# Two of sixteen weight pieces converted inside the last feed-forward instead of the expert slots

## The chip, the cores and the metric

One core of one Trainium2 chip runs the whole program. The metric is the device time of one execution in microseconds (us); the profile is one execution taken by the hardware profiler. TensorE is PE in the profile (PEld is its weight load), VectorE is DVE, ScalarE is ACT, GpSimd is POOL, SyncE is SP.

## The reference

Three layers follow each other. Attention over q, k, v (4 x 8 heads x 576 x 64) with a position bias gives x of 2304 x 512. A mixture of 8 experts sends each row to one expert:

```python
h = np.maximum(x[mask] @ w1[e], 0.0)
out[mask] = gate_w[mask, None] * (h @ w2[e])
```

The last feed-forward, with `w_in` 512 x 2048 and `w_out` 2048 x 512 that the host hands over as 64-bit floats, is

```python
r = np.maximum(x @ w_in, 0.0)
g = r * r
return (g @ w_out).astype(np.float32)
```

## The kernel before

**Stages.** Attention runs first. Then 22 expert slots (`run_slots`, L1283), each 128 rows of one expert; then the last feed-forward (L1381 to L1521) in 9 blocks of 256 rows. Matrix products are done in pairs of 16-bit halves: every operand has a high half and a low half, and a product is three products of halves.

**An expert slot.** PE does `ff1` for the next slot in two parts of 48 matmuls (L1220), transposes of x for the slot after it (L1203), and `ff2` of this slot, 24 matmuls (L1235). ACT and DVE make the halves of the results (L1225, L1226, L1243), and, where the expert changes, of the next first weight (`split_w1`, L1014 and L1015). POOL gathers rows and scatters results by DMA and splits x. SP loads first weights (L999, four DMAs of 512 KB), second weights (L1008, four DMAs of 512 KB into one buffer `vt`, each as soon as `ff2` has read the old quarter).

**The conversion in the slots.** The 64-bit weights have to become 16-bit halves. `convert(i, ...)` (L1101) does one of 16 pieces: pieces 0 to 7 are `w_in`, 8 to 15 are `w_out`. A `w_out` piece is a load of 1 MB by SP (L1109), then in this order Abs on ACT (L1116), a clamp and a shift on DVE (L1118, L1119), two bit operations on DVE (L1121, L1123), four subtractions on POOL (L1136) that make the 7 combinations of a fast 2 x 2 block product, the high half on ACT (L1140), the low half on DVE (L1142), and a store by SP into a DRAM buffer `wosc` (L1144). `pieces` (L1147) interleaves the pieces in steps, seven per piece; `piece(t, n)` (L1278), called four times per slot, issues steps until `1 + (t - 2 + 0.25 n) * CPACE` are done, with `CPACE` 6.1. All engines run their queues in the order written in the program.

**The last feed-forward.** SP loads the eight pieces of `w_out` from `wosc` into the resident tile `woh` (L1503). `g_unit(j, c)` (L1411) is one unit: PE makes two column groups of x @ w_in (24 matmuls, L1420) into one of four PSUM buffers, ACT does relu (L1426) into `gf`, of which there are two. Every second unit closes a pair: a square (L1431 on ACT in blocks 0 and 1, L1433 on DVE later), four adds on POOL (L1436), and then for the pair before it the high half on ACT (L1443) and the low half on DVE (L1444) into the block's tile `g2` (28 KB per partition, two buffers). `ff2_of(j)` (L1446) is the second product of block j, seven products of 24 matmuls (`prod`, L1454) that each run over all eight pieces of `woh`, piece 7 last. Its first product (`pf_a`) stands ahead of unit 13 (block 1, c = 5), the next two ahead of units 14 and 15, the other four after unit 15. So units 0 to 12 have no second product between them.

```python
if c > (2 if j > 1 else 4) and not (last and c == 6):
    next(two, None)
g_unit(j, c)
```

Of the kernel before, what the change touches and what calls it, by code (L numbers as in the profile page):

```python
# [7 lines left out]
F32 = mybir.dt.float32  # L8
F16 = mybir.dt.float16
U32 = mybir.dt.uint32  # L10
I32 = mybir.dt.int32
AF = mybir.ActivationFunctionType
ALU = mybir.AluOpType
# [10 lines left out]
P = 128  # L24
# [14 lines left out]
W1S, W2S, YS = 64.0, 64.0, 2.0 ** -8  # L39
WIS, RS, WOS = 64.0, 2.0 ** -8, 64.0  # L40
OUTS = 2.0 ** -22
CPACE = 6.1
NCONV, NWIN = 16, 8
HSW = 134
TINY64, HUGE = 2.0 ** -15 * 1.125, 3e38

# [37 lines left out]
def body(ctx: ExitStack, tc: tile.TileContext, q, k, v, wsm, emb, tau, mw1, mw2, win, wout, cst_d, lsk_d, ids_d, out):  # L84
    nc = tc.nc
    win, wout = win.bitcast(U32), wout.bitcast(U32)
    PE, ACT, DVE, POOL, SP = nc.tensor, nc.scalar, nc.vector, nc.gpsimd, nc.sync
# [863 lines left out]
    with tc.manual_schedule():  # L951
# [149 lines left out]
        def convert(i, wrp):  # L1101
            wr = wrp.tile([P, 1024, 2], U32, name="wr2", bufs=4)
            wf = wr.rearrange("p n t -> p (n t)")
            if i < NWIN:
                kc, n = divmod(i, 2)
                SP.dma_start(out=wf, in_=win[kc * P:(kc + 1) * P, n * 2048:(n + 1) * 2048])
            else:
                g = i - NWIN
                SP.dma_start(out=wf, in_=wout[g * P:(g + 1) * P, :])  # L1109
            lo, hi = wr[:, :, 0], wr[:, :, 1]  # L1110
            yield
            tb = wrp.tile([P, 8, 256], F32, name="tb", bufs=2)
            flat = tb.rearrange("p q n -> p (q n)")
            af, bf = flat[:, :1024], flat[:, 1024:]
            b = bf.bitcast(U32)
            ACT.activation(bf, hi.bitcast(F32), AF.Abs)  # L1116
            yield
            DVE.tensor_scalar(bf, bf, TINY64, None, op0=ALU.max)  # L1118
            DVE.tensor_scalar(b, b, 3, 0x3FFFFFF8, op0=ALU.logical_shift_left, op1=ALU.bitwise_and)  # L1119
            yield  # L1120
            DVE.scalar_tensor_tensor(out=b, in0=lo, scalar=29, in1=b, op0=ALU.logical_shift_right, op1=ALU.bitwise_or)  # L1121
            yield
            DVE.scalar_tensor_tensor(out=af.bitcast(U32), in0=hi, scalar=0xC0000000, in1=b,  # L1123
                                     op0=ALU.bitwise_and, op1=ALU.bitwise_or)
            yield
            if i < NWIN:
                yield
                dh, dl = (wih[:, a, kc, n * 1024:(n + 1) * 1024] for a in range(2))
                ACT.activation(dh, af, AF.Copy, scale=WIS)
                yield  # L1130
                DVE.scalar_tensor_tensor(out=dl, in0=af, scalar=WIS, in1=dh, op0=ALU.mult, op1=ALU.subtract)
                yield
                return
            for d, x, y, op in ((4, 0, 1, ALU.subtract), (5, 2, 4, ALU.subtract), (6, 2, 0, ALU.subtract),
                                (7, 3, 5, ALU.subtract)):
                POOL.tensor_tensor(out=tb[:, d], in0=tb[:, x], in1=tb[:, y], op=op)  # L1136
            yield
            wo = wf.bitcast(F16)[:, :2 * 7 * 256]
            dh, dl = wo[:, :7 * 256], wo[:, 7 * 256:]
            ACT.activation(dh, flat[:, 256:], AF.Copy, scale=WOS)  # L1140
            yield
            DVE.scalar_tensor_tensor(out=dl, in0=flat[:, 256:], scalar=WOS, in1=dh, op0=ALU.mult, op1=ALU.subtract)  # L1142
            yield
            SP.dma_start(out=wosc[:, g * 3584:(g + 1) * 3584], in_=wo)  # L1144


        def pieces(cs):  # L1147
            for c in cs[:4]:
                next(c)
            yield  # L1150
            next(cs[0])
            yield
            none = iter(())
            for n in range(len(cs) + 1):
                c, d = cs[n] if n < len(cs) else none, cs[n - 1] if n else none
                next(c, None)
                if 0 < n <= NWIN and n + 3 < len(cs):
                    next(cs[n + 3])
                yield
                next(d, None)  # L1160
                yield
                next(c, None)
                yield
                next(d, None)
                if n > NWIN + 1 and n + 2 < len(cs):
                    next(cs[n + 2])
                yield
                next(c, None)
                yield
                next(c, None)  # L1170
                if n + 1 < len(cs):
                    next(cs[n + 1])
                yield
                next(d, None)
                yield
# [7 lines left out]
        wrp = ep("e_wr", 1)  # L1183
# [77 lines left out]
            DVE.tensor_copy(orow[:, i:i + 1], yr[:, DM + 1:XW])  # L1261


        conv = pieces([convert(i, wrp) for i in range(NCONV)])
        done = [0]
        state = ["tail"]
        yq, yd = [], []
# [10 lines left out]
        def piece(t, n):  # L1278
            while done[0] < (1 if t < 2 else 1 + (t - 2 + 0.25 * n) * CPACE):
                next(conv, None)  # L1280
                done[0] += 1
# [99 lines left out]
        with ExitStack() as fctx:  # L1381
            fp = lambda n, bufs, **kw: tp(fctx, n, bufs, **(kw if "space" in kw else dict(side="right")))
            woh = fp("f_wo", 1).tile([P, 8, 2, 7, 256], F16, name="woh")
            gp = fp("f_g", 2)
# [7 lines left out]
            gts, gfs, late, outs = {}, {}, [], []  # L1392
            yv = lambda j: y0[:, :, :, 256 * (j % 2):256 * (j % 2) + 256]

            def y_load(j):
                for i in range(2):
                    t = 2 * j + i
                    SP.dma_start(out=us_t[t % 4][:, :XW], in_=y_d[t * P:(t + 1) * P, :])
# [11 lines left out]

            def g_unit(j, c):  # L1411
                y2 = yv(j)
                if c == 0:
                    gts[j] = gp.tile([P, 2, 7, 8, P], F16, name="g2")
                p_ = pf1.tile([P, 2, 256], F32, name="pf1")
                for h in range(2):
                    f, i = 8 * h + c, 0
                    for kc in range(4):
                        for a, b in ((0, 0), (0, 1), (1, 0)):
                            PE.matmul(p_[:, h], lhsT=wih[:, a, kc, f * P:(f + 1) * P], rhs=y2[:, b, kc, :],  # L1420
                                      start=(i == 0), stop=(i == 11))
                            i += 1
                if c % 2 == 0:
                    gfs[j] = gfp.tile([P, 8, 2, P], F32, name="gf")
                g = gfs[j]
                ACT.activation(g[:, 0:4, c % 2, :], p_.rearrange("p h (i n) -> p (h i) n", i=2), AF.Relu, scale=RS)  # L1426
                if c % 2 == 0:
                    return
                g4 = g[:, 0:4].rearrange("p q c n -> p (q c n)")
                if j < 2:  # L1430
                    ACT.activation(g4, g4, AF.Square)  # L1431
                else:
                    DVE.tensor_tensor(out=g4, in0=g4, in1=g4, op=ALU.mult)  # L1433
                for d, x, y, op in ((4, 0, 2, ALU.add), (5, 4, 1, ALU.subtract), (6, 1, 0, ALU.subtract),
                                    (7, 3, 5, ALU.subtract)):
                    POOL.tensor_tensor(out=g[:, d], in0=g[:, x], in1=g[:, y], op=op)  # L1436
                g_split()
                late.append((g, gts[j], c - 1))

            def g_split():  # L1440
                while late:
                    g, gt, c = late.pop()
                    ACT.copy(gt[:, 0, :, c:c + 2, :], g[:, 1:8])  # L1443
                    DVE.tensor_tensor(out=gt[:, 1, :, c:c + 2, :], in0=g[:, 1:8], in1=gt[:, 0, :, c:c + 2, :], op=ALU.subtract)  # L1444
# [54 lines left out]
                put(0)  # L1499
                yield  # L1500

            for g in range(8):
                SP.dma_start(out=woh[:, g].rearrange("p a q n -> p (a q n)"), in_=wosc[:, g * 3584:(g + 1) * 3584])  # L1503
            for j in range(NB):
                two = ff2_of(j - 1) if j else iter(())
                last = j == NB - 1
                for c in range(8):
                    if c > (2 if j > 1 else 4) and not (last and c == 6):
                        next(two, None)
                    g_unit(j, c)  # L1510
                    if 0 < j < NB - 1:
                        if c == 0:
                            y_load(j + 1)
                        if c in (3, 5):
                            y_split(2 * (j + 1) + c // 2 - 1)
                if last:
                    g_split()
                for _ in two:
                    pass
# [68 lines left out]
```

## Time and profile before

| what | us |
|---|---|
| three timed runs, median (lowest to highest) | 1030.5 (1030.4 to 1036.81) |
| profiled execution, its own time | 1023.01 |
| span of the profiled execution | 1021.2 |
| PE busy in it | 949.9 (93%) |
| DVE, ACT, POOL busy | 657.3, 541.0, 500.6 |
| expert slots with conversion, by the trace | about 427 to 655 |
| units 0 to 12 of the last feed-forward | 655 to 689 |

The profiled execution lies 1.8 us above its span and 7.5 us below the median of the timed runs. PE's ends are modelled, so a busy PE is not a PE at its peak: how long a fixed number of matmuls takes is the better reading.

### The profile page before, as it was taken

What the parts mean: (1) busy time and instruction counts of PE and PEld (TensorE: products, weight loads), DVE (VectorE), ACT (ScalarE), POOL (GpSimd) and SP (SyncE); (2) the same over time, 40 slices, a digit from 0 to 9 for tenths busy, and PEclk for the clock granted to TensorE, in tenths of its full rate; (3) what the DMA queues carried; (4) which work ended last, traced back from release to release, by engine and by line L of the source; (5) the groups of instructions that cost most, each with busy time, mean ns of one, the idle gap of its engine ahead of it and who ended that gap; (6) DMA issues with size and microseconds to landing.
All of it is one profiled execution on the core that took longest, in us unless ns stands there. A gap on an engine that the chain in (4) does not pass through costs nothing. (4 is left out here: it accounts for less than half of the span.)

```text
span 1021.2 us, 24809 instructions
## 1 busy us (share of the span) xinstructions
PE 949.9 (93%) x9725; PEld 751.8 (74%) x9725; DVE 657.3 (64%) x1229; ACT 541.0 (53%) x1000; POOL 500.6 (49%) x415
## 2 busy tenths in 40 slices
PE   7587899999899889999989899999999999999995
PEld 4355676677677767776667677688888888888884
DVE  6665789899988764677866768235455555545441
ACT  5575677777877673466656564355333233333330
POOL 1212537356433352366638798266454654645541
PEclk9798999999999989999989999999999999999998
DMA  8989886898789334599899484371121111021001
GB/s 285 309 242 294 283 262 201 263 283 292 225 254 324 145 126 148 222 333 334 327 370 336 148 288 156 114 301 42 32 54 42 31 53 42 27 58 22 21 2 42
DMA packets 78843, 187.17 MB, mean 183 GB/s; under 512 B 26648, under 2 KB 26776, under 8 KB 76128
## 3 DMA queue, kind: packets, MB, share of 16 engines
q1 hardware_dynamic: 72656, 169.98, 49.8%
q0 software_dynamic: 6064, 15.54, 4.4%
q8 instruction: 78, 1.28, 0.5%
q14 instruction: 45, 0.37, 0.1%
HBM read 171.65 MB, written 51.73 MB: 219 GB/s over the span
## 5 line engine op out<-in xcount | busy, mean ns | idle before, releaser
L1436 POOL TENSOR_TENSOR gf<-gf 128x256 f32<-128x256 f32 x144 | 165.9, 1171 | 146.7 <-DVE gf L1433 124.4
L1420 PE MATMUL pf<-big,wih 128*128 128x256 f16 x1728 | 196.0, 273 | 1.8 <-PEq L1374 1.8
L1420 PEld LDWEIGHTS <-wih 128*128 128x128 f16 x1728 | 169.0, 98 | 21.8 <-issue 2.2
L1458 PEld LDWEIGHTS <-g 128*128 128x128 f16 x1512 | 147.4, 98 | 18.7 <-issue 1.0
L1426 ACT ACTIVATE gf<-pf 128x512 f32<-128x512 f32 x72 | 42.5, 597 | 193.6 <-PE pf L1420 138.0
L1220 PE MATMUL ph<-x,w1b 128*128 128x128 f16 x2112 | 127.1, 220 | 7.2 <-DVEq L1024 2.5
L1220 PEld LDWEIGHTS <-w1b 128*128 128x128 f16 x2112 | 121.7, 99 | 12.3 <-DVEq L1024 3.0
L471 POOL TENSOR_TENSOR wh<-wr,w2s_c 128x1024 f16<-128x1024 f32 x32 | 61.1, 1910 | 133.8 <-DMA wr<-in_mw_dram 71.1
L1235 PE MATMUL py<-vt,h 128*128 128x512 f16 x528 | 120.3, 385 | 5.3 <-DMA vt<-wsc 5.3
L522 ACT ACTIVATE pr<-ssb,mn 128x576 f32<-128x576 f32 x144 | 111.7, 776 | 12.8 <-DVE mn L509 12.5
L1444 DVE TENSOR_TENSOR g<-gf,g 128x1792 f16<-128x1792 f32 x36 | 85.5, 2374 | 50.3 <-ACT g L1443 50.3
L509 DVE CUSTOM_DVE_ANT_0 ssb<-ps_s,bias 128x576 f32<-128x576 f32 x144 | 107.4, 748 | 8.7 <-DMA bias<-bias_d 7.0
L498 PE MATMUL ps_s<-kst,qd 128*128 128x288 f16 (+1 forms) x640 | 97.4, 293 | 10.8 <-DVE mn L509 9.1
L1433 DVE TENSOR_TENSOR gf<-gf 128x1024 f32<-128x1024 f32 x28 | 34.3, 1225 | 113.6 <-ACT gf L1426 113.6
L1235 PEld LDWEIGHTS <-h 128*128 128x128 f16 x528 | 51.5, 99 | 65.3 <-issue 9.7
L531 PE MATMUL ps_t<-cst,pr 128*128 128x128 f32 x576 | 93.3, 286 | 1.2 <-DVE pt L209 1.0
L556 PE MATMUL pv<-pt,vt 128*64 128x128 f32 (+1 forms) x1280 | 85.5, 277 | 6.6 <-DMA vt<-in_v_dram 5.7
L556 PEld LDWEIGHTS pv<-pt,vt 128*64 128x64 f32 x1280 | 68.0, 142 | 23.3 <-issue 16.4
L531 PEld LDWEIGHTS ps_t<-cst,pr 128*128 128x128 f32 x576 | 65.7, 146 | 24.0 <-issue 19.8
L498 PEld LDWEIGHTS <-qd 128*128 128x128 f16 (+1 forms) x640 | 56.9, 102 | 26.0 <-issue 16.6
L1443 ACT CAST g<-gf 128x1792 f16<-128x1792 f32 x36 | 60.3, 1676 | 4.3 <-POOL gf L1436 4.3
L207 ACT COPY pt<-ps_t 128x512 f32<-128x512 f32 x99 | 57.0, 576 | 10.3 <-PE ps_t L531 10.2
(194 smaller groups left out, 1542.7 us busy)
## 6 DMA issues: line engine op xcount, KB each, us to landing
vt<-wsc SPq DMA_DIRECT2D x88, 512.0 KB
wr<-in_mw_dram SPq DMA_DIRECT2D x76, 512.0 KB
kst<-in_mw_dram SPq DMA_DIRECT2D x44, 512.0 KB
wsc<-wh SPq DMA_DIRECT2D x32, 512.0 KB
bias<-bias_d SPq DMA_DIRECT2D x16, 576.0 KB
bias_d<-rt SPq DMA_DIRECT2D x28, 295.5 KB
qd<-qh SPq DMA_DIRECT2D x64, 128.0 KB
wr<-in_win_dram SPq DMA_DIRECT2D x8, 1024.0 KB
```

What stands on the lines that cost most here:

```text
L471: POOL.tensor_tensor(out=wh[:, 0], in0=wr, in1=w2s_c.to_broadcast([P, 1024]), op=ALU.mult)
L498: PE.matmul(s[r, hf, :288], lhsT=qd[:, h2, i, pr, r], rhs=kst[x - x % 2][:, pr, h2, x % 2, js], start=(i == 0), stop=(i == 1))
L509: DVE.tensor_tensor_reduce(out=ss.rearrange("p (a j) -> p a j", a=2), in0=s[:, :, :288], in1=btile[bkey[u]][:, h2].rearrange("p (a j) -> p ...
L522: ACT.activation(pr_sb[k_ // 2][:, h2], ssb.pop(k_), AF.Exp, bias=mns.pop(k_), scale=-1.0, accum_out=sums[c, b][:, h:h + 1])
L531: PE.transpose(pt_ps[k_][:, jc * P:(jc + 1) * P], src[:, j0:j0 + P], eye)
L556: PE.matmul(pv[o, cs], lhsT=vb[:, 2 * jc + h2, d] if jc < 4 else vb[o, 8, d], rhs=a[h2][:, jc, cs] if jc < 4 else e[o, cs], start=(jc == 0 ...
L1220: PE.matmul(p_[:, f4, :], lhsT=w[:, a, kc, f * P:(f + 1) * P], rhs=x2[:, b, kc, :], start=(i == 0), stop=(i == 11))
L1235: PE.matmul(p_, lhsT=h2[:, a, fc, :], rhs=wb2[fc // 2][:, b, fc % 2, :], start=(i == 0), stop=(i == 23))
L1420: PE.matmul(p_[:, h], lhsT=wih[:, a, kc, f * P:(f + 1) * P], rhs=y2[:, b, kc, :], start=(i == 0), stop=(i == 11))
L1436: POOL.tensor_tensor(out=g[:, d], in0=g[:, x], in1=g[:, y], op=op)
L1444: DVE.tensor_tensor(out=gt[:, 1, :, c:c + 2, :], in0=g[:, 1:8], in1=gt[:, 0, :, c:c + 2, :], op=ALU.subtract)
L1458: PE.matmul(ps, lhsT=gt[:, a, s, c, :], rhs=woh[:, c, b, w, :], start=(i == 0 and first), stop=(i == 23 and end), skip_group_check=True)
```

## The change

The last two pieces of `w_out` (6 and 7 of 8) are taken out of the slots; the other 14 pieces are spread over the same slots with `CPACE` 5.4. The two are loaded raw into the second `g2` buffer, ahead of the `woh` loads in SP's queue, and are converted in the first units of the last feed-forward with the same operations, straight into `woh`; their stores to and loads from `wosc` fall away. All the scratch is in that buffer: two raw pieces and one work area for both. `finish_step` is called after each unit, twice where the block is 0 or 1, from unit 4 on.

```diff
-CPACE = 6.1
-NCONV, NWIN = 16, 8
+CPACE = 5.4
+NCONV, NWIN, NLATE = 16, 8, 2
...
-        conv = pieces([convert(i, wrp) for i in range(NCONV)])
+        conv = pieces([convert(i, wrp) for i in range(NCONV - NLATE)])
...
-            for g in range(8):
+            for j in range(2):
+                gts[j] = gp.tile([P, 2, 7, 8, P], F16, name="g2")
+            spare = gts[1].rearrange("p a q c n -> p (a q c n)").bitcast(U32)
+            rows = [spare[:, 2048 * i:2048 * i + 2048] for i in range(NLATE)]
+            for i in range(NLATE):
+                g = 8 - NLATE + i
+                SP.dma_start(out=rows[i], in_=wout[g * P:(g + 1) * P, :])
+            flat = spare[:, 4096:6144].bitcast(F32)
+            def finish(i):
...
+                ACT.activation(bf, hi.bitcast(F32), AF.Abs)
+                yield
+                DVE.tensor_scalar(bf, bf, TINY64, None, op0=ALU.max)
+                DVE.tensor_scalar(b, b, 3, 0x3FFFFFF8, op0=ALU.logical_shift_left, op1=ALU.bitwise_and)
+                yield
+                DVE.scalar_tensor_tensor(out=b, in0=lo, scalar=29, in1=b, op0=ALU.logical_shift_right, op1=ALU.bitwise_or)
+                yield
+                DVE.scalar_tensor_tensor(out=af.bitcast(U32), in0=hi, scalar=0xC0000000, in1=b,
+                                         op0=ALU.bitwise_and, op1=ALU.bitwise_or)
+                yield
...
+                    POOL.tensor_tensor(out=tb[:, d], in0=tb[:, x], in1=tb[:, y], op=op)
+                yield
+                dh, dl = (woh[:, 8 - NLATE + i, a].rearrange("p q n -> p (q n)") for a in range(2))
+                ACT.activation(dh, flat[:, 256:], AF.Copy, scale=WOS)
+                yield
+                DVE.scalar_tensor_tensor(out=dl, in0=flat[:, 256:], scalar=WOS, in1=dh, op0=ALU.mult, op1=ALU.subtract)
+                yield
+            ends = [x for i in range(NLATE) for x in [finish(i)]]
+            def finish_step(u):
+                if u >= 4 and ends and next(ends[0], 0) == 0:
+                    ends.pop(0)
+                    if ends:
+                        next(ends[0])
+            for g in range(8 - NLATE):
                 SP.dma_start(out=woh[:, g].rearrange("p a q n -> p (a q n)"), in_=wosc[:, g * 3584:(g + 1) * 3584])
...
                     g_unit(j, c)
+                    finish_step(8 * j + c)
+                    if j < 2:
+                        finish_step(8 * j + c)
```

## Rows read from the trace of the kernel before

**Rows 1.** Busy time by stretch: us; PE, PEld, DVE, ACT, POOL; PEclk, DMA share, GB/s.

```profile
427.30:655.20 227.90, 215.53 (x2379) 155.10 (x2376) 162.64 (x200) 128.24 (x158) 149.45 (x127) 0.98 0.74 273
655.20:691.90 36.70, 36.67 (x336) 32.92 (x337) 10.29 (x4) 17.92 (x21) 22.22 (x21) 1.00 0.58 227
```

**Rows 2.** What PE waited for, 427 to 656: us in total, times, longest.

```profile
PE py L1235 <- DMA vt<-wsc: 5.3, 3, 3.7
PE ph L1220 <- DVEq L1024: 2.1, 2, 1.7
PE ph L1220 <- DVE w1b L1015: 2.0, 2, 1.4
...
PE ph L1220 <- ACT w1b L1014: 1.3, 1, 1.3
```

**Rows 3.** Timeline of PE in the slots: start, us, what [idle before <- releaser].

```profile
483.76 5.34 PE L1235 MATMUL py<-vt,h 128*128 128x512 f16 x24 [1.39 <-DMA vt<-wsc]
...
521.00 8.21 PE L1235 MATMUL py<-vt,h 128*128 128x512 f16 x24 [3.66 <-DMA vt<-wsc]
...
580.49 3.59 PE L1220 MATMUL ph<-x,w1b 128*128 128x128 f16 x40 [0.63 <-DVE w1b L1015]
...
596.75 2.84 PE L1220 MATMUL ph<-x,w1b 128*128 128x128 f16 x48
```

**Rows 4.** Busy time by stretches of 5 us around that wait, columns as in rows 1.

```profile
495.00:500.00 5.00, 5.00 (x26) 2.29 (x25) 4.17 (x5) 5.00 (x6) 4.18 (x4) 1.00 0.30 66
...
520.00:525.00 5.00, 4.00 (x10) 1.43 (x10) 4.96 (x6) 1.76 (x2) 0.55 (x1) 0.50 1.03 410
```

**Rows 5.** Timeline of SP: loads of raw weight pieces in the slots.

```profile
497.77 0.35 SPq L1109 DMA_DIRECT2D wr<-in_wout_dram  x1
...
506.63 0.37 SPq L1109 DMA_DIRECT2D wr<-in_wout_dram  x1
```

**Rows 6.** Conversion's work tile: ns min/median/max of one, first and last start, forms.

```profile
L1136 POOL TENSOR_TENSOR tb<-tb x32: 715/726/1746, 553.9 to 647.8; 128x256 f32<-128x256 f32 x32
L1116 ACT ACTIVATE tb<-wr x16: 1130/1155/1188, 428.7 to 633.4; 128x1024 f32<-128x1024 f32 x16
L1118 DVE TENSOR_SCALAR tb<-tb x16: 676/683/1269, 430.3 to 634.5; 128x1024 f32<-128x1024 f32 x16
...
L1121 DVE SCALAR_TENSOR_TENSOR tb<-wr,tb x16: 1207/1219/1630, 432.0 to 636.9; 128x1024 uint32<-128x1024 uint32 x16
...
L1140 ACT ACTIVATE wr<-tb x8: 1689/1697/1697, 556.8 to 648.8; 128x1792 f16<-128x1792 f32 x8
L1142 DVE SCALAR_TENSOR_TENSOR wr<-tb,wr x8: 2010/2016/2973, 562.2 to 650.5; 128x1792 f16<-128x1792 f32 x8
```

**Rows 7.** Timeline of ACT ahead of PE's waits at 577.

```profile
572.97 1.70 ACT L1140 ACTIVATE wr<-tb 128x1792 f16<-128x1792 f32 x1 [4.67 <-POOL tb L1136]
...
576.56 3.89 ACT L1014 ACTIVATE w1b<-wr 128x1024 f16<-128x1024 f32 x4
```

**Rows 8.** Timeline of all engines in the first units of the last feed-forward.

```profile
655.23 34.22 PE L1420 MATMUL pf<-big,wih 128*128 128x256 f16 x312 [1.78 <-PEq L1374]
...
674.12 4.68 POOL L1436 TENSOR_TENSOR gf<-gf 128x256 f32<-128x256 f32 x4 [1.76 <-ACT gf L1431]
675.65 2.57 DVE L1444 TENSOR_TENSOR g<-gf,g 128x1792 f16<-128x1792 f32 x1 [3.88 <-ACT g L1443]
678.31 1.08 ACT L1426 ACTIVATE gf<-pf 128x512 f32<-128x512 f32 x2 [2.70 <-DVE g L1444]
...
684.76 1.09 ACT L1426 ACTIVATE gf<-pf 128x512 f32<-128x512 f32 x2 [2.70 <-DVE g L1444]
...
688.54 2.57 DVE L1444 TENSOR_TENSOR g<-gf,g 128x1792 f16<-128x1792 f32 x1 [3.87 <-ACT g L1443]
689.29 2.78 PE L1458 MATMUL pf_a<-woh,g 128*128 128x256 f16 x24
...
691.91 2.78 PE L1420 MATMUL pf<-big,wih 128*128 128x256 f16 x24
```

More of the change, by code (lines that the diff above doesn't have):

```diff
@@ L1412, in g_unit @@
                 y2 = yv(j)
-                if c == 0:
+                if c == 0 and j not in gts:
                     gts[j] = gp.tile([P, 2, 7, 8, P], F16, name="g2")
@@ new lines, in finish @@
+            def finish(i):
+                wr = rows[i].rearrange("p (n t) -> p n t", t=2)
+                lo, hi = wr[:, :, 0], wr[:, :, 1]
+                tb = flat.rearrange("p (q n) -> p q n", q=8)
+                af, bf = flat[:, :1024], flat[:, 1024:]
+                b = bf.bitcast(U32)
+                ACT.activation(bf, hi.bitcast(F32), AF.Abs)
[8 more added lines that the diff above has]
+                yield
+                for d, x, y, op in ((4, 0, 1, ALU.subtract), (5, 2, 4, ALU.subtract), (6, 2, 0, ALU.subtract),
+                                    (7, 3, 5, ALU.subtract)):
+                    POOL.tensor_tensor(out=tb[:, d], in0=tb[:, x], in1=tb[:, y], op=op)
[5 more added lines that the diff above has]
+                yield
```

## The prediction, made before the changed kernel was run

> **What bounds the kernel now.** I read the busy time by stretch first. In the slots with conversion PE is busy 215.5 of 227.9 us at a granted clock of 0.98, in the first units of the last feed-forward 36.67 of 36.70 us at 1.00, while DVE, ACT and POOL have idle time in both [rows 1]. So PE sets the pace on both sides of the change, and the other engines count only where they make PE wait. What PE waited for in the slots is short: 5.3 us for the second weights' DMAs and 2.1 + 2.0 + 1.3 = 5.4 us for DVE and ACT [rows 2]. To that comes half clock after a wait. 24 matmuls that take 5.34 us took 8.21 behind a wait of 3.66 us [rows 3], with a granted clock of 0.50, which is 1.2 GHz [rows 4]: 2.9 us. Behind the waits at 577, 40 matmuls took 3.59 us, where 48 take 2.84 and so 40 take 2.37 [rows 3]: 1.2 us. All that the slots can give back is 5.3 + 5.4 + 2.9 + 1.2 = 14.8 us.
>
> In the last feed-forward I looked for slack. PE does 13 units of 24 matmuls in 34.22 us, 2.63 us each. ACT, DVE and POOL go round in a loop of 6.45 us per two units: relu of the next pair stands 2.70 us until DVE's low half of the pair before last is done (678.31 to 684.76 is one turn) [rows 8]. That is slower than PE's 5.26, and four PSUM buffers are the cover. It is all but used up at unit 13: the first second product starts at 689.29 and needs column groups 6 and 7 of `g2` after 18 of its 24 matmuls, at 691.25; DVE ends them at 688.54 + 2.57 = 691.11 [rows 8]. PE has 0.14 us to spare there, so whatever delays that loop stops PE.
>
> **The slots: what goes.** Two pieces leave, each with 5.8 us of DVE, 2.9 of ACT, 2.9 of POOL [rows 6], a load, a store and a later load. Of this only what stands in PE's waits is worth anything. A piece takes seven steps, so at 5.4 steps per slot instead of 6.1 it spans 1.30 slots instead of 1.15, and each step comes later, by 0.75 slot around slot 8 and by more than one slot around slot 13. Counted out, two things change.
>
> DMA: the queue was nearly empty before 500 (66 GB/s) and full after it (410 GB/s at 520) [rows 4]. From then until the second weights of slot 10 were in, it had two raw pieces (their loads were issued at 497.77 and 506.63 [rows 5]), one set of first and two of second weights: 1.05 + 1.05 + 3 x 2.10 = 8.4 MB, 20.5 us at 410 GB/s, which gives 520.5 against 521.0 measured. After the change the second of these loads is due in slot 10.0 instead of 9.25, behind the weights that PE waits for, so 1.05 MB less is ahead of them, 2.6 us. The wait of 3.66 falls to about 1.1 and the half clock behind it goes, and what is left of the 5.3 (0.2) goes, because the first of the two loads moves behind the weights of slot 9. The wait of 1.39 at 483.76 [rows 3] stays: the same loads are ahead of it. Gain 0.2 + 2.6 + 2.9 = 5.7; bounds 0 and 8.2.
>
> Engines: ACT stood 4.67 us for POOL before the high half of a `w_out` piece, and the new expert's first weights were queued behind that at 576.56 [rows 7], which PE then waited for. That high half was due at slot 14.0; after the change the one near it falls to 14.25, behind the weights in ACT's queue, and between slots 12.0 and 15.0 POOL gets one piece instead of three. I take 5.3 of 5.4 + 1.2 = 6.6; bounds 0 (other steps meet the same spots) and 6.6. The slots give back 11.0 us, between 0 and 14.8.
>
> **The last feed-forward: what comes.** DMA adds nothing. The two raw loads are 2.1 MB against 1.8 MB of `woh` loads that go; at 410 GB/s they take 5 us, and the first of them is wanted at 672. SP issues them ahead of the `woh` loads, 0.35 us each [rows 5], and `woh` is first read at 689.
>
> The engines' queues decide. I walk them with the durations of rows 6 and 8 and 0.1 us for each handover; without the additions the same walk ends relu 8 at 685.4 and the low half of pair 3 at 691.2, against 685.3 and 691.1 in the trace [rows 8]. With them, by unit:
>
> Unit 4: relu, then Abs of piece 6 on ACT to 673.6, clamp and shift to 675.0. Unit 5: square and pair 1's high half on ACT to 676.8, its low half on DVE to 679.4, then the two bit operations to 681.9. Unit 6: relu 6 to 680.0; POOL's four subtractions 681.9 to 684.8; the high half of piece 6 is ACT's next instruction and waits for them, 4.9 us, with relu 7, a square and pair 2's high half queued behind it. It ends at 686.6. Unit 7: relu 7 ends 687.2 instead of 679.4, pair 2's low half 692.5, then piece 6's low half 694.5; Abs of piece 7 must wait for that, as both pieces have one work area, and ends 695.7. Unit 8: relu 8 waits behind it and ends 696.3 instead of 685.4; clamp, shift, first bit operation to 698.4. Unit 9: square and pair 3's high half to 699.5, its low half to 702.1, the second bit operation 703.4, POOL 706.3. Unit 10: the high half of piece 7 to 708.1, its low half to 710.2.
>
> PE: unit 11 waits for relu 7 (3.1 us), unit 12 for relu 8 (6.5 us), and the first second product, which reads all eight pieces, has its last three matmuls waiting for the low half of piece 7 at 710.2. It ends at 710.6; the next unit began at 691.91 before [rows 8]. That is 18.7 us, and nothing later gives it back, as PE has no gap after it. The last wait is 7.8 us long, so half clock comes behind it; priced by the row of 3.66 us [rows 3], 2.9. The waits before it bring half clock too, but what runs slower there ends ahead of 710.2 anyway. Sum 21.6 us. Bounds of the queues: if POOL and DVE never slow each other (POOL's four at 2.9 instead of 4.68, the low half at 2.03 instead of 2.57), the walk ends at 708.5, 16.5 us late, and 0 for the clock is the low end; if POOL's subtractions take 4.68 each time, 22.3, with 2.9 for the clock 25.2.
>
> A rule of the Trainium skill weighs on the half clock. The page "TensorE: Matmul & The Clock Gate", section "Why this matters for your kernels", ties the fall to 1.2 GHz to one long idle gap between bursts. By that the gap of 7.8 us costs as I price it, but the waits at 577, none over 1.4 us, would cost none, and the slots could give back 13.6 instead of 14.8. The trace shows 3.59 us for 40 matmuls there, so I keep the row.
>
> **The sum.** -11.0 + 21.6 = +10.6 us. The profiled execution would go from 1023.0 to 1033.6; the timed median is 7.5 above the profiled one, and I move it by the same 10.6, from 1030.5 to 1041.1.
>
> **The rivals.** A, the slots give nothing back: the pieces' steps meet other expert changes, and the DMA queue, full from 500 to 530, waits as long. For it: only two of the waits are traced to conversion work by rows. Gain 2, so 1030.5 - 2 + 21.6 = 1050.1. B, both ends in the change's favour: the slots give all of 14.8, the queues cost their low 16.5 without half clock: 1032.2. C, the other side, not slower: the added work fills idle time. From 655 to 692 DVE is idle 26.4 us and ACT 18.8 [rows 1], and two pieces need 11.6 and 5.7. If ACT's waits on POOL fall where ACT would stand anyway, only the pieces' own chain counts: 2 x 11.6 us from 672.4 gives 695.6 against 691.6 needed, 4.0 us late. That makes 1030.5 - 11.0 + 4.0 = 1023.5. It decides at the end of piece 7's low half: ahead of 703 the change doesn't lose. Against it: the queues are in order, and ACT's next instruction behind each wait is a relu that PE needs. D, that the change doesn't do what it says, I see no way for: each piece is needed by every product.
>
> **How the numbers follow.** Forecast 0.50, with its own range 1034 to 1048 (cost 18.7 to 25.2, gain 7.5 to 15). A 0.17, B 0.23, C 0.10. The range to hold eight times in ten, 1025 to 1050, reaches nearly to C and to A. One per cent, about what a measurement of this kernel can tell from no change, is 10.3 us: 1020.2 and 1040.8. Slower by over that: A 0.16 and a little over half of the forecast, 0.29, together 0.45. Faster by over that: C with all that the slots can give (4.0 - 14.8 = -10.8) and the unknown, 0.05. Within: 0.50.
>
> **What would show it.** Right: PE waits at units 11 and 12 for ACT's relu and in `pf_a` for DVE's write of `woh`, 16 to 19 us together, with a clock of 0.5 behind it; piece 7's low half ends 55 us after the first unit's start; ACT stands 4 to 5 us for POOL before a piece's high half; from 427 to the first unit is shorter by 8 to 14 us; the stretch after unit 16 is unchanged. Wrong: no wait in `pf_a`, or PE's waits in the slots as long as before.

## The result, and the profile after

Nine timed runs of each kernel gave a median of 1035.31 us (1032.06 to 1041.83) after and 1028.95 (1021.09 to 1036.81) before. The ratio on record, estimated from the runs, is 1.0097 with a 95% interval of 1.0069 to 1.0125: 1029 x 0.0097 = 10.0 us slower, between 7.1 and 12.9, where 10.6 was forecast. The two medians themselves lie only 6.4 us apart (1.0062), so the size of the loss is known to some 3 us and no better. The profiled execution took 1035.43 us, with a span of 1033.6.

Spans of two executions can't be set against each other here as they stand. The first 48 expert matmuls began at 392.03 us before and at 397.05 after, and between 383 and 397 in the executions below, though nothing that precedes them was edited. So I compare two stages: the slots, from that start to unit 0's, and the head of the last feed-forward, from unit 0 to the second product's second part (`pf_b`).

| stage, us | before | after | change |
|---|---|---|---|
| slots (392.03 to 655.23; 397.05 to 646.58) | 263.20 | 249.53 | -13.67 |
| unit 0 to `pf_b` (to 694.53; to 706.91) | 39.30 | 60.33 | +21.03 |
| unit 0 to unit 16 (to 715.49; to 727.87) | 60.26 | 81.29 | +21.03 |

The last two rows agree, and from unit 16 to the end of the span it is 305.7 us in both, so nothing after `pf_b` gives the loss back or adds to it. The two stages add up to +7.4 us; the other 5.0 of the 12.4 by which the two spans differ lie ahead of the slots. What PE waited for from 427 to 720 in the kernel after (us in total, times, longest):

```profile
PE pf L1420 <- ACT gf L1426: 8.3, 2, 5.1
PE pf_a L1458 <- ACT woh L1532: 5.3, 1, 5.3
PE pf_a L1458 <- DVE woh L1534: 1.7, 1, 1.7
PE py L1235 <- DMA vt<-wsc: 1.3, 4, 0.5
PE ph L1220 <- issue: 0.9, 2, 0.5
PE pf L1420 <- PEq L1374: 0.4, 1, 0.4
PE px L1203 <- POOL xs L1038: 0.4, 1, 0.4
PE ph L1220 <- DVE sl_Y L948: 0.3, 1, 0.3
```

The first three lines are new, 15.3 us, all of it in the head. The DMA line is 5.3 us in [rows 2], and the three lines of DVE and ACT there, 5.4 us, have no counterpart left. PE's timeline after, at the spot of the long DMA wait and in the head (start, us, what [idle before <- releaser]):

```profile
523.33 1.46 PE L1235 MATMUL py<-vt,h 128*128 128x512 f16 x6 [0.18 <-DMA vt<-wsc]
525.16 4.04 PE L1235 MATMUL py<-vt,h 128*128 128x512 f16 x18 [0.37 <-DMA vt<-wsc]
...
646.58 28.98 PE L1420 MATMUL pf<-big,wih 128*128 128x256 f16 x264 [0.44 <-PEq L1374]
678.77 4.27 PE L1420 MATMUL pf<-big,wih 128*128 128x256 f16 x24 [3.21 <-ACT gf L1426]
688.14 4.70 PE L1420 MATMUL pf<-big,wih 128*128 128x256 f16 x24 [5.09 <-ACT gf L1426]
692.67 2.46 PE L1458 MATMUL pf_a<-woh,g 128*128 128x256 f16 x21
700.45 0.37 PE L1458 MATMUL pf_a<-woh,g 128*128 128x256 f16 x1 [5.32 <-ACT woh L1532]
702.51 0.59 PE L1458 MATMUL pf_a<-woh,g 128*128 128x256 f16 x2 [1.69 <-DVE woh L1534]
702.89 4.19 PE L1420 MATMUL pf<-big,wih 128*128 128x256 f16 x24
706.91 2.78 PE L1458 MATMUL pf_b<-woh,g 128*128 128x256 f16 x24
```

At 523 the wait is 0.18 + 0.37 us and the 24 matmuls take 1.46 + 4.04, where [rows 3] have 3.66 and 8.21. In the head eleven units run undisturbed (264 matmuls), then units 11 and 12 wait for ACT's relu, and the last three of 24 matmuls of `pf_a` for piece 7's two halves. Three groups of 24 take 4.27, 4.70 and 4.19 us instead of 2.78.

Busy time by stretch after, columns as in [rows 1]: the slots, the head, and two stretches of 5 us that answer to [rows 4]:

```profile
427.00:646.60 219.60, 216.23 (x2475) 158.20 (x2473) 150.09 (x203) 125.30 (x158) 129.13 (x120) 1.00 0.72 264
646.60:706.90 60.30, 44.98 (x360) 37.65 (x361) 26.32 (x18) 28.20 (x32) 33.95 (x33) 0.86 0.40 154
500.00:505.00 5.00, 5.00 (x41) 2.88 (x38) 3.44 (x4) 3.99 (x6) 4.14 (x5) 1.00 0.54 191
520.00:525.00 5.00, 4.60 (x63) 3.61 (x61) 2.92 (x5) 3.94 (x6) 2.28 (x3) 1.00 1.03 405
```

The slots are down to 3.4 us in which PE is not busy and a granted clock of 1.00. In the head PE is idle 15.3 us of 60.3, beside engines that are each busy about half of it: no engine is full, so the order of the queues is the suspect, and e8 tests it. The last stretch was at 0.50 before and is at 1.00.

The other engines' timeline in the head after shows how:

```profile
673.61 2.90 POOL L1529 TENSOR_TENSOR g<-g 128x256 f32<-128x256 f32 x4 [2.42 <-DVE g L1524]
676.54 1.70 ACT L1532 ACTIVATE woh<-g 128x1792 f16<-128x1792 f32 x1 [5.24 <-POOL g L1529]
678.14 0.58 ACT L1426 ACTIVATE gf<-pf 128x512 f32<-128x512 f32 x1
...
683.91 2.54 DVE L1534 SCALAR_TENSOR_TENSOR woh<-g,woh 128x1792 f16<-128x1792 f32 x1
686.48 1.12 ACT L1517 ACTIVATE g<-g 128x1024 f32<-128x1024 f32 x1 [5.09 <-DVE woh L1534]
687.49 1.08 ACT L1426 ACTIVATE gf<-pf 128x512 f32<-128x512 f32 x2
...
689.74 6.09 POOL L1436 TENSOR_TENSOR gf<-gf 128x256 f32<-128x256 f32 x4 [5.17 <-ACT gf L1431]
...
695.79 2.88 POOL L1529 TENSOR_TENSOR g<-g 128x256 f32<-128x256 f32 x4
...
698.70 1.70 ACT L1532 ACTIVATE woh<-g 128x1792 f16<-128x1792 f32 x1 [4.43 <-POOL g L1529]
...
700.43 2.03 DVE L1534 SCALAR_TENSOR_TENSOR woh<-g,woh 128x1792 f16<-128x1792 f32 x1 [5.18 <-ACT woh L1532]
```

ACT stands 5.24 us for POOL's subtractions, and the relu that PE needs is the next entry of its queue (678.14). It stands 5.09 us for piece 6's low half before it may take the absolute value of piece 7 (L1517), and the relu at 687.49 is next again. Then 4.43 us for POOL, with `pf_a` waiting for the result.

### The profile page after: what moved, and what is told of

Its sections match the earlier page's. It is cut to its first block, busy times and chain, and to the rows that moved or that the text cites. A ratio compares the mean times of both kernels' runs of the same rounds, so it can differ in the third digit from the quotient of the medians.

```text
span 1033.6 us, 24806 instructions
## 1 busy us (share of the span) xinstructions
PE 950.9 (92%) x9725; PEld 750.4 (73%) x9725; DVE 658.3 (64%) x1229; ACT 541.1 (52%) x1000; POOL 487.4 (47%) x415
## 5 line engine op out<-in xcount | busy, mean ns | idle before, releaser
L1420 PE MATMUL pf<-big,wih 128*128 128x256 f16 x1728 | 201.1, 276 | 8.7 <-ACT gf L1426 8.3
L1420 PEld LDWEIGHTS <-wih 128*128 128x128 f16 x1728 | 171.4, 99 | 31.6 <-issue 9.6
L522 ACT ACTIVATE pr<-ssb,mn 128x576 f32<-128x576 f32 x144 | 111.8, 776 | 13.8 <-DVE mn L509 13.6
L1235 PE MATMUL py<-vt,h 128*128 128x512 f16 x528 | 117.7, 379 | 1.3 <-DMA vt<-wsc 1.3
L531 PEld LDWEIGHTS ps_t<-cst,pr 128*128 128x128 f32 x576 | 65.4, 145 | 24.2 <-issue 19.7
L1226 DVE SCALAR_TENSOR_TENSOR h<-ph,h 128x512 f16<-128x512 f32 x44 | 30.4, 690 | 58.7 <-ACT h L1225 39.1
```

The lines of the kernel that those rows point to most:

```text
L522: ACT.activation(pr_sb[k_ // 2][:, h2], ssb.pop(k_), AF.Exp, bias=mns.pop(k_), scale=-1.0, accum_out=sums[c, b][:, h:h + 1])
L531: PE.transpose(pt_ps[k_][:, jc * P:(jc + 1) * P], src[:, j0:j0 + P], eye)
L1235: PE.matmul(p_, lhsT=h2[:, a, fc, :], rhs=wb2[fc // 2][:, b, fc % 2, :], start=(i == 0), stop=(i == 23))
```

## Experiments

Each run was timed beside the kernel before on the same chip, and stages are read as above. Where a variant moves `pf_a`, unit 0 to unit 16 stands in for the head. The slots as the change has them took 249.5 to 251.6 us in five executions (after, e1, e5, e6, e8), those of the kernel before 263.2 and 262.0 (before, e2), so a stage of one execution is good to about 2 us. Edits are shown shortened to the part of a line that changes.

| run | slots | unit 0 to `pf_b` | unit 0 to 16 | ratio to before (interval) |
|---|---|---|---|---|
| before | 263.20 | 39.30 | 60.26 | |
| after | 249.53 | 60.33 | 81.29 | 1.0097 (1.0069 to 1.0125) |
| e1 slots alone | 250.86 | 39.30 | | 0.9897 (0.9870 to 0.9924) |
| e2 head alone | 262.01 | 61.42 | | 1.0203 (1.0168 to 1.0239) |
| e3 less work, old pace | 262.22 | 39.29 | | 0.9977 (0.9950 to 1.0005) |
| e4 earlier start | 258.89 | 39.29 | | 0.9966 (0.9936 to 0.9997) |
| e5 subtractions on DVE, head | 249.74 | 57.29 | 78.25 | 1.0083 (1.0048 to 1.0117) |
| e8 other order, head | 249.47 | 52.84 | 73.80 | 0.9996 (0.9961 to 1.0030) |
| e6 e5 and e8, `pf_a` later | 251.56 | | 67.34 | 0.9950 (0.9919 to 0.9982) |
| e7 one piece late | 260.94 | | 62.39 | 0.9981 (0.9946 to 1.0016) |
| e9 all 16, faster late | 255.15 | | 65.4 | 0.9994 (0.9961 to 1.0026) |
| e10 one late, other order | 250.98 | | 66.9 | 0.9972 (0.9946 to 0.9998) |
| e12 subtractions on DVE, slots | 257.51 | | 60.26 | 0.9934 (0.9895 to 0.9973) |
| e13 e12 at a later pace | 252.87 | 39.30 | | 0.9863 (0.9828 to 0.9899) |

**e1 and e2: the two sides apart.** e1 is the kernel before with the slots of the change alone: it leaves out the conversion of pieces 6 and 7 of `w_out` and loads 0 and 1 in their place. e2 is the change with the old slots: all 16 pieces are converted there, and 6 and 7 once more in the head.

```diff
 # e1, on the kernel before
-CPACE = 6.1
+CPACE = 5.4
-conv = pieces([convert(i, wrp) for i in range(NCONV)])
+conv = pieces([convert(i, wrp) for i in range(NCONV - 2)])
-in_=wosc[:, g * 3584:(g + 1) * 3584]
+in_=wosc[:, g % 6 * 3584:(g % 6 + 1) * 3584]
 # e2, on the kernel after
-CPACE = 5.4
+CPACE = 6.1
-range(NCONV - NLATE)
+range(NCONV)
```

> The slots' part of the change alone: 14 pieces at 5.4 steps per slot, nothing converted in the last feed-forward (weight pieces 6 and 7 are not converted; woh gets pieces 0 and 1 a second time). Theory (the change is a gain in the slots and a larger loss in the first units, and the two just add): the stretch from the first expert matmul to unit 0 takes 249.5 us as after the change (263.2 before), the stretch from unit 0 to the second product pf_b takes 39.3 as before, the time falls by 13.7, ratio near 0.987. Rival (most of the slots' gain in the one profile is that execution's luck): 257 to 263 us and a ratio of 0.995 to 1.000.

> The first units' part alone: all 16 pieces in the slots at 6.1 steps per slot as before, and pieces 6 and 7 converted a second time in the first units, from where woh gets them. Theory: slots 263 us as before, unit 0 to pf_b 60.3 us instead of 39.3, the time rises by 21, ratio near 1.020. Rival (the slots gain nothing that lasts and the 10 us measured are all that the first units cost): unit 0 to pf_b 50 us, ratio 1.010.

e1 gained 1.03% and e2 lost 2.03%; their sum, +1.00%, matches the +0.97% of the whole. The stages say the same: -12.3 us in e1's slots, +22.1 in e2's head. So the two sides hardly touch, and both gain and loss are real.

**e3: is the gain the work left out?** e1 with the old pace, so again without pieces 6 and 7.

```diff
-CPACE = 5.4
+CPACE = 6.1
```

> 14 pieces at the old 6.1 steps per slot, nothing converted in the last feed-forward (pieces 6 and 7 are not converted; woh gets pieces 0 and 1 a second time). Every step up to piece 13 stands where it stood before; only slots 18 to 21 get lighter. Theory (the gain in the slots is where the steps fall, not how many there are): PE's waits in slots 7 to 16 are as before, first expert matmul to unit 0 takes 261 to 265 us, ratio 1.000. Rival (the gain is the work left out): 250 to 256 us, ratio 0.988 to 0.993.

The slots shortened by 1.0 us, and the interval of the ratio holds 1. What PE waited for from 380 to 655 in e3 is nearly [rows 2]:

```profile
PE py L1235 <- DMA vt<-wsc: 4.0, 2, 2.3
PE ph L1220 <- DVEq L1024: 3.0, 3, 2.1
PE ph L1220 <- ACTq L1024: 2.1, 2, 1.3
PE ph L1220 <- DVE w1b L1015: 1.8, 2, 1.2
```

Two pieces fewer bring next to nothing at the old pace; of e1's gain nearly all comes with the slower pace, which shifts the other steps.

**e12: the engines' part.** The kernel before, with the four subtractions of a piece on DVE (L1136).

```diff
-POOL.tensor_tensor(out=tb[:, d], in0=tb[:, x], in1=tb[:, y], op=op)
+DVE.tensor_tensor(out=tb[:, d], in0=tb[:, x], in1=tb[:, y], op=op)
```

> The kernel before with one edit: the four subtractions of each w_out piece in the slots on DVE instead of POOL, steps as before. Theory (of the slots' waits, 6.6 us are ACT standing for POOL ahead of a high half): PE's waits for DVE and ACT at 560 to 595 go or shrink to under 2 us, the waits for the second weights stay at 4 to 5.5 us; first expert matmul to unit 0 takes 256 to 259 us, ratio 0.993 to 0.997. Rival (DVE's load sets those waits): they stay at 5 us or grow, 262 us or more, ratio 0.999 or above.

What ACT waited for from 550 to 652, first before, then in e12:

```profile
ACT wr L1140 <- POOL tb L1136: 13.6, 4, 5.0
```

```profile
ACT wr L1140 <- DVE tb L1136: 1.1, 1, 1.1
```

And what PE waited for from 427 to 660 in e12:

```profile
PE py L1235 <- DMA vt<-wsc: 4.8, 2, 3.6
PE ph L1220 <- issue: 2.1, 5, 0.5
PE pf L1420 <- PEq L1374: 1.6, 1, 1.6
```

ACT's standing for the subtractions fell from 13.6 to 1.1 us, and with it every wait of PE for DVE and ACT from 427 on; the DMA waits, untouched, stayed. All that was expected came. That is the split the prediction made: engine waits, from ACT's queue, and DMA waits, from the order of the loads. Its engine part was 5.3 us, and e12's slots are 5.7 us shorter.

**e4 and e9: other paces with all 16 pieces.** e4 begins two slots earlier and goes slower; e9 goes at 5.4 and catches up late.

```diff
 # e4
-CPACE = 6.1
+CPACE = 5.55
-while done[0] < (1 if t < 2 else 1 + (t - 2 + 0.25 * n) * CPACE):
+while done[0] < 1 + (t + 0.25 * n) * CPACE:
 # e9
-CPACE = 6.1
+CPACE = 5.4
-while done[0] < (1 if t < 2 else 1 + (t - 2 + 0.25 * n) * CPACE):
+x = t - 2 + 0.25 * n
+while done[0] < 1 + max(x, 0) * CPACE + max(x - 15, 0) * 2.85:
```

> All 16 pieces in the slots, none late, but the steps begin in slot 0 instead of slot 2, at 5.55 per slot instead of 6.1. Theory (slower steps meet fewer of PE's deadlines, whatever their number): first expert matmul to unit 0 takes 250 to 257 us instead of 263.2, ratio 0.988 to 0.995, with no cost in the first units. Rival (the two pieces that left are what made room): 262 to 266 us, ratio 1.000 or above, as slots 0 to 2 also carry the end of attention.

> All 16 pieces in the slots, none late: 5.4 steps per slot up to slot 17 as in the changed kernel, then 8.25 to the end. Theory (the slots gain by where the steps fall up to slot 17, and slots 17 to 21 had room): first expert matmul to unit 0 takes 250 to 255 us, unit 0 to pf_b 39.3, time 8 to 12 us below the kernel before, ratio 0.988 to 0.993. Rival (8.25 steps per slot make ACT stand for POOL in slots 17 to 21 and PE behind it): 258 us or more, ratio 0.996 or above.

Both missed. e4 gained 4.3 us in the slots; its DMA wait fell to 1.6 us, but from 427 on PE still waited 4.5 us for ACT and DVE (5.4 before), and 2.5 for POOL's split of x (L1038), a wait that the kernel before doesn't show. e9 gained 8.1 in the slots and lost 5.1 behind them, as the hurried end of the conversion still held ACT when unit 0 began: ACT stood 5.78 us for POOL ahead of the last high half, which ran to 654.7, and PE waited 3.0 us for ACT there. What a pace brings depends on where each step falls, and I couldn't foretell it from the pace.

**e5, e8 and e6: can the head hold two pieces?** e5 moves the four subtractions of `finish` to DVE. e8 gives the steps other units, so that piece 6 starts after unit 3 and piece 7 after unit 7, and ACT's high halves come after units 5 and 9, which close a pair. e6 does both and starts `pf_a` one unit later.

```diff
 # e5
-POOL.tensor_tensor(out=tb[:, d], in0=tb[:, x], in1=tb[:, y], op=op)
+DVE.tensor_tensor(out=tb[:, d], in0=tb[:, x], in1=tb[:, y], op=op)
 # e8
-finish_step(8 * j + c)
-if j < 2:
-    finish_step(8 * j + c)
+for _ in range(plan.get(8 * j + c, 0)):
+    next(ends, None)
 # with
+ends = (x for i in range(NLATE) for x in finish(i))
+plan = {3: 3, 4: 2, 5: 1, 6: 1, 7: 2, 8: 3, 9: 1, 10: 1}
 # e6: both, and
-if c > (2 if j > 1 else 4) and not (last and c == 6):
+if c > (2 if j > 1 else 5) and not (last and c == 6):
```

> The changed kernel with one edit: the four subtractions of the two late pieces on DVE instead of POOL, at the same places. Theory (the queues: ACT stands for POOL ahead of each high half, and the relu that PE needs stands behind it): the walk of the queues gives a loss of 15.6 us where it gave 18.7, so unit 0 to pf_b falls from 60.3 to about 57, ACT's two waits on POOL of 5 us become waits of 1 to 3 us on DVE; time 3 us below the changed kernel, ratio to before about 1.006. Rival (the chain of the pieces alone or the DVE's load sets the loss): 60 us or more, ratio 1.010 or above.

> The changed kernel with the same operations on the same engines and only the places of the 14 late steps changed: 3 in unit 3, 2 in 4, 1 in 5, 1 in 6, 2 in 7, 3 in 8, 1 in 9, 1 in 10. Theory (places in the in-order queues): the walk gives a loss of 6.8 us instead of 18.7, so unit 0 to pf_b about 46 to 48, ratio to before 0.995 to 0.999. Rival (the amount of work, or POOL and DVE slowing each other): still above 56 us, ratio 1.006 or above.

> The same two late pieces, three edits against the changed kernel: subtractions on DVE; the 14 steps start in unit 3 and are laid out by hand (3 in unit 3, 2 in 4, 1 in 5, 1 in 6, 2 in 7, 3 in 8, 1 in 9, 1 in 10); the first second product one unit later (block 1, c = 6). Theory (only the order in the queues costs, the work fits): the walk gives a loss of 1.7 us, so unit 0 to the end of unit 15 is within 3 us of the kernel before; with the slots' 249 to 251 us the time falls by 8 to 12 us, ratio 0.988 to 0.993. Rival (the work does not fit beside the units whatever the order): PE waits 8 us or more, ratio 1.000 or above.

e5 hit its 57 us (57.29), though ACT still stood 3.86 and 3.01 us, now for DVE, where 1 to 3 were expected. e8 cut the head's loss from 21.0 to 13.5 us with the same instructions on the same engines: this other order alone takes off a third. But its 52.84 us are 4.8 above the range, neither what the theory nor what the rival said, and 6.7 above the walk; 2.4 of that is half clock behind the last wait (24 matmuls in 5.15 us). e6 lost 7.1 us where at most 3 were expected. The pieces' chains were longer than walked. POOL's timeline in e8, then DVE's in e5 and in e6:

```profile
653.87 4.60 POOL L1529 TENSOR_TENSOR g<-g 128x256 f32<-128x256 f32 x4 [3.89 <-DVE g L1524]
```

```profile
661.86 1.55 DVE L1529 TENSOR_TENSOR g<-g 128x256 f32<-128x256 f32 x4
```

```profile
655.46 1.21 DVE L1519 TENSOR_SCALAR g<-g 128x1024 f32<-128x1024 f32 x1
...
660.36 2.90 DVE L1529 TENSOR_TENSOR g<-g 128x256 f32<-128x256 f32 x4
```

The same four subtractions took 2.90 us on POOL after (673.61) and 4.60 in e8; on DVE 1.55 and 2.90; the clamp of L1519 0.68 [rows 6] and 1.21. In the slow cases the other of the two engines was at work in the same microseconds. The walks of e6, e7 and e8 fell short by 2 to 7 us, of which this explains a part.

**e7 and e10: one piece late.** Both take only piece 7 into the head, with 15 in the slots.

```diff
 # e7, on the kernel after
-CPACE = 5.4
+CPACE = 5.72
-NCONV, NWIN, NLATE = 16, 8, 2
+NCONV, NWIN, NLATE = 16, 8, 1
 # and e8's edit with
+plan = {3: 2, 4: 2, 6: 1, 7: 1, 8: 1}
 # e10: e7 with
+CPACE = 5.4
+x = t - 2 + 0.25 * n
+while done[0] < 1 + max(x, 0) * CPACE + max(x - 15, 0) * 1.36:
+plan = {3: 1, 4: 1, 6: 2, 8: 1, 9: 1, 10: 1}
+if c > (2 if j > 1 else 5) and not (last and c == 6):
```

> Only one late piece (7), 15 pieces in the slots at 5.72 steps per slot; the late piece's steps are 2 in unit 3, 2 in 4, 1 each in 6, 7 and 8, subtractions on POOL as in the changed kernel. Theory: the walk gives no loss at all in the first units (39.3 us from unit 0 to pf_b), and the slots give part of their 13 us, 4 to 9: ratio 0.991 to 0.996. Rival (any piece converted there stops PE): unit 0 to pf_b 45 us or more.

> One late piece, its steps 1 each in units 3, 4, 8, 9 and 10 and 2 in unit 6, the first second product one unit later; 15 pieces in the slots at 5.4 steps per slot up to slot 17, then 6.76. Theory: a walk of the queues in which DVE and POOL never run their two-operand instructions at the same moment gives no loss in the first units (60.3 us from unit 0 to unit 16 as before), the slots take 250 to 255 us; ratio 0.988 to 0.993. Rival (a late piece always costs some 2 us as it did in the run with one): 62 to 63 us there, ratio 0.990 to 0.995.

Both missed. e7's head lost 2.1 us, against none expected, and its pace gave back only 2.3 in the slots: there PE waited 5.0 us for POOL's split of x. e10's slots gained 12.2, but its head lost 6.7: the later `pf_a` put the second products in a row, and `pf_c` met DVE's combination late, in PE's timeline

```profile
701.99 4.45 PE L1459 MATMUL pf_c<-woh,g 128*128 128x256 f16 x24 [3.18 <-DVE u L1464]
```

3.18 us of wait and 4.45 - 2.78 = 1.7 of slow matmuls. Moving the first product to make room had been costed at nothing. Two waits for ACT, 0.62 us ahead of unit 1 and 0.57 ahead of unit 12, bring it to 6.0 of the 6.7.

**e13: a version that beats both.** e12, the load pace of the change up to slot 11, faster from there, so that all 16 pieces end in the slots.

```diff
 # e12 and
-CPACE = 6.1
+CPACE = 5.4
-while done[0] < (1 if t < 2 else 1 + (t - 2 + 0.25 * n) * CPACE):
+x = t - 2 + 0.25 * n
+while done[0] < 1 + max(x, 0) * CPACE + max(x - 9, 0) * 1.25:
```

> All 16 pieces in the slots, none late, subtractions of the w_out pieces on DVE, 5.4 steps per slot up to slot 11 and 6.65 after it. Theory (two causes that add: ACT standing for POOL, gone with the subtractions on DVE; and the DMA queue in slots 7 to 10, eased by the later loads): waits for the second weights 1 to 3 us in all instead of 5.3, waits for DVE and ACT under 2 us, first expert matmul to unit 0 takes 250 to 254 us, unit 0 to pf_b 39.3; ratio 0.987 to 0.992, below every version so far that computes everything. Rival (7.25 us of DVE per piece at 6.65 steps per slot make DVE the bound): 257 us or more, ratio 0.994 or above.

The ratio is 0.9863 (0.9828 to 0.9899), 14 us faster than before (10 to 18), a little more than expected; the slots account for 10.3 of it. Set beside 1.0097 that is about 24 us faster than the change, though the two were not timed side by side. PE's waits from 427 to 656 in e13:

```profile
PE pf L1421 <- PEq L1375: 1.8, 1, 1.8
PE py L1235 <- DMA vt<-wsc: 1.5, 3, 0.7
PE px L1203 <- POOL xs L1038: 1.4, 1, 1.4
PE ph L1220 <- issue: 0.9, 2, 0.5
```

The waits for ACT and DVE that e12 took away stay away, and those for the second weights are down from 4.8 us in e12 to 1.5. The slots take 252.87 us, 4.6 less than in e12, where the prediction put 5.7 on the DMA part, and the head is at its 39.30. So what the change gained in the slots doesn't need the two pieces moved. No run has this pace with the subtractions left on POOL.

## Why the prediction was right, step by step

**The forecast held in sign and place, and in size as far as the runs can tell.** +10.6 was forecast; the ratio gives +10.0, the medians +6.4, the two stages +7.4. The total alone can't tell the forecast from rival B: the median of 1035.31 lies 5.8 below the 1041.1 of the forecast and 3.1 above B's 1032.2. The two sides measured apart can. A needs slots that give 2 us, and e1 alone gained 1.03%, 10.5 us. B needs a head that costs 16.5 with no half clock behind it, and C one 4 us late; it is 21 late, with half clock.

**The slots: 11.0 forecast; 13.7 in the profile, 10.5 timed in e1.** The DMA part went as counted. Piece 9's load (506.63 in [rows 5]) is now issued behind the weights that PE wants at 523.33, as SP's timeline after shows: the raw load of 529.02 comes after the issues of 513.63.

```profile
508.62 0.34 SPq L1109 DMA_DIRECT2D wr<-in_wout_dram  x1
510.58 2.64 SPq L999 DMA_DIRECT2D wr<-in_mw_dram  x4
513.63 4.08 SPq L1008 DMA_DIRECT2D vt<-wsc  x4
...
529.02 0.34 SPq L1109 DMA_DIRECT2D wr<-in_wout_dram  x1
```

The raw load before 508.62 was issued at 496.40, ahead of the stretch of 191 GB/s, so one raw piece and not two stands in the full queue. The wait fell to 0.55, where 1.1 was forecast, and the half clock went. "The wait of 1.39 stays" was half true: it is 0.30 + 0.49 after, but 1.71 in e1, at the same pace. The engine part came too, with ACT's high half behind the weights, as forecast:

```profile
569.95 3.88 ACT L1014 ACTIVATE w1b<-wr 128x1024 f16<-128x1024 f32 x4
573.73 1.68 ACT L1140 ACTIVATE wr<-tb 128x1792 f16<-128x1792 f32 x1
```

PE's waits in the slots fell from 12.5 to 3.3 us, 9.2 less; with half clock of 2.9 + 1.2 that makes 13.3 of the 13.7. Of it 1.3 was not in my sum, the wait on PE's own sequencer (PEq) ahead of unit 0: 1.78 in [rows 8], now 0.44. By the rule of the Trainium skill ("TensorE: Matmul & The Clock Gate", section "Why this matters for your kernels") that ties half clock to one long gap, the 1.2 at 577 would not count and 12.1 be explained. 13.7 stands nearer to the sum with it, but 1.2 us is no more than the scatter of executions. The granted clock of the kernel before decides: in the 3.59 us behind those three waits, none over 1.4 us, it is 0.64 (busy time by stretch, columns as in [rows 1]), so the clock did fall there without one long gap, and the row was the better guide.

```profile
580.49:584.08 3.59, 3.59 (x43) 3.59 (x44) 3.59 (x3) 0.45 (x1) 0.88 (x1) 0.64 0.19 73
```

**The head: 21.6 forecast, 21.0 measured.** The walk put the low half of piece 7 55 us after unit 0, and it ended at 700.43 + 2.03 - 646.58 = 55.9. Unit 11's wait came to 3.21 (3.1 forecast), unit 12's to 5.09 (6.5), and those in `pf_a` to 5.32 + 1.69 = 7.0 (9.1, what is left of the 18.7). The sum, 15.3 for 18.7, is smaller because units 11 and 12 ran at half clock, which moved 1.5 + 1.9 us from waits into matmuls, as "what runs slower there ends ahead of 710.2 anyway" had it. One term was mis-sized: half clock behind the last wait cost 4.19 - 2.78 = 1.4, not 2.9. It was in part made up by a queue that ended 0.9 later, where DVE and POOL slowed each other: POOL's four adds at 689.74 took 6.09 us beside DVE's work, where [rows 8] have 4.68, and piece 7's subtractions stood behind them until 695.79. One reading was off, with no weight in the sum: `pf_a` wants DVE's low half after 20 of its 24 matmuls and not after 18 (it stops there in e7 and e8), so PE had 0.36 us to spare at unit 13 and not 0.14. How much of the loss is queue order: a third goes by placing the same steps elsewhere (e8), 3.0 go with POOL's subtractions on DVE (e5), for which ACT had stood 5.24 + 4.43 us, and with both and a later `pf_a` two thirds are gone (e6, 7.1 left). Whether the last third is order too, no run shows.

**What was luck.** That 10.6 and 10.0 lie so close is luck, with an interval of some 3 us to either side: in the profile the slots gave 2.7 us more than forecast and the head took 0.6 less, so the two stages make 7.4. The walk of the change fell right because DVE and POOL met there mostly as in the trace that the durations come from: POOL's adds took 4.68, 4.69, 4.68 and 6.09 us where [rows 8] have 4.68, its subtractions 2.90 and 2.88 where [rows 6] give 2.9. Walks of the variants were 2 to 7 us short in e6, e7, e8 and e10. So the method holds to some 1 us for a schedule whose overlaps resemble those in the trace from which the durations come, and not beyond. Still open: why POOL's split of x came late in e4 and e7, each with a pace between the old and the new, where part of their gain went.

## What to carry to other kernels

Idle time of an in-order engine can't be filled by the microsecond: walk the queues, and ask of each added instruction which engine feeds it and what stands behind it, here a relu that PE needs behind a high half that waits for POOL. When removed work shortens a stage, test whether the work or the shift of everything else did it (e3); if it was the shift, look for a way to have the shift without moving the work. It took a second edit here (e13), and two other paces by themselves failed (e4, e9). Four subtractions moved onto the engine that produces their inputs, and loads issued a little later, gained 1.4% where the change as a whole lost 1.0%.

## What the runs showed of the hardware

DVE and POOL held each other up: four 128x256 subtractions or adds on POOL took 2.88 to 2.90 us alone and 4.60 to 6.09 beside DVE's work, four subtractions on DVE 1.55 alone (e5) and 2.90 beside POOL's (e6), and even a DVE clamp with one input took 1.21 (e6) for 0.69 (after). The Trainium skill's page "GPSIMD Engine Reference", section "Key points", says that the two share their ports to SBUF and contend when DVE runs in its two-port mode or reads two SBUF inputs. The durations of the subtractions agree, and put a size to it; whether the clamp ran in that mode, no trace shows.

Half clock did not follow the length of one wait: after a wait of 3.21 us for relu 7, unit 11 ran at a granted clock of 0.52 in the kernel after, which is 1.2 GHz nearly throughout, and after 3.23 us at the same place in e2 at 1.00. In the windows of busy time of the two kernels, after and then e2:

```profile
678.80:682.00 3.20, 3.20 (x16) 2.29 (x16) 0.51 (x1) 2.58 (x2) 2.04 (x3) 0.52 0.00 0
```

```profile
685.20:687.90 2.70, 2.70 (x24) 2.32 (x24) 0.00 (x0) 2.60 (x2) 1.52 (x3) 1.00 0.00 0
```

So a price for half clock behind a wait of that size is uncertain by 1.5 us: 24 matmuls took 4.27 us in the one and 2.78 in the other.
